# Second matrix of the early expert: loaded into the first one's buffers as they are split, split behind the token table

## The chip, the cores and the metric

One core of a Trainium2 chip runs one program. Its engines work side by side, each through a queue of its own: TensorE (PE, with its weight loads PEld), VectorE (DVE), ScalarE (ACT), GpSimd (POOL) and SyncE (SP), which here issues nearly all transfers between memory and the core's buffers. The metric is the device time of the program in microseconds (us), the median of the timed runs.

## The reference: what is computed

Three stages follow each other on 2304 tokens (4 batches x 576 positions) of 512 features:

```python
# attention: a downsampled one (mean of 4 positions) and a local band of +-3 positions
out_up = np.repeat(sm_attn(q_d, k_d, v_d), 4, axis=2)
out_local = np.matmul(softmax(mask(scale * q @ k.T)), v)
x = out_up + out_local                       # -> (2304, 512)
# mixture of 8 experts, one per token
logits = x @ w_gate + modality_bias[modality_id]
e_idx = np.argmax(logits, axis=1); gate_w = softmax(logits)[e_idx]
for e in range(8):                           # w1: 512x1024, w2: 1024x512 each
    out[mask] = gate_w * (np.maximum(x[mask] @ w1[e], 0.0) @ w2[e])
# dense layer, 512 -> 2048 -> 512, with softplus between
g = np.maximum(h, 0.0) + np.log1p(np.exp(-np.abs(h)))   # h = x @ w_in
return g @ w_out
```

All tensors are float32.

## The kernel before

**Precision and splits.** A float32 product is made of three products: each operand is split into a high part `wh` (an ACT copy into a shorter type, L332) and a low part `wl` (a DVE subtraction of `wh` from the raw value, L333). A weight matrix of an expert (2 MB) is loaded and split in four *quarters* of 128 x 1024 values (512 KB). A quarter is loaded by SP into one of eight raw buffers, raw0 to raw7, split from there into a ring of `wh`/`wl` pairs, and the raw buffer is then free for the next load.

**Slots.** Behind the gate the tokens are gathered by expert into slots of 128 rows. A slot s runs `gemm1` (24 matmuls against w1, `h` = its result behind a ReLU, L582), `h_t` (PE turns h, L1149; ACT and DVE split it into `hh` and `hl`, L526 and L527) and `gemm2` (24 matmuls against w2; ACT writes the result `y`, L1170, SP stores it to `ys`, L1172). Slots 0 and 1 belong to the *early expert*: the one with the most tokens after half of them have been gated. Its w1 is loaded and split while the attention of the last tokens still runs (step "W" of phase A), and its 8 quarters serve both slots. From slot 2 on the expert comes from a table `widx` that the last gate group makes. SP reads `widx` into registers (L283, for two mixed slots L311) and issues the loads under a condition (L289, L290), which leaves a load out where a slot has the same expert as the one before.

**The order.** The list `parts` gives the order in which quarters are loaded and split: parts 0 to 3 are the early expert's w1, 4 to 7 its w2, 8 to 11 w1 of slot 2, 12 to 15 w1 of slot 3, 16 to 19 w2 of slot 2, and so on. Products ask for their quarters through `part`, which splits up to two quarters ahead; `split_part` also loads up to eight ahead as far as buffers are free. The function `raw_of` says which raw buffer a quarter uses: in the slots w1 takes raw4 to raw7 and w2 raw0 to raw3. The buffers raw4 to raw7 exist from the start; raw0 to raw3 belong to a pool that opens behind phase A. Within one engine's queue a scheduler may move instructions by its own estimate, except those that are marked with `keep_in_program_order`, which keep their order among themselves.

**The last gate group.** The tokens 13*128 to 18*128 are the last gate group. For a tile PE turns x (L833), ACT copies it (`xT`, L834), PE multiplies it with the gate's weights (L845), ACT copies that (`lT`, L847), PE collects (L848); DVE then makes the logits (`lg`, L861), the maximum (`gmx`, L864), `ex` (L867) and the counts; PE sums them (L888), and DVE goes on to the token table (`tokt`, L935) and to `widx` (L412). `tables` turns the token table into the lists `gidx` by which POOL gathers the slots' rows (`xg`, L521). The attention's loads `up` (L767, added to x by POOL, L821) are in SP's queue at the same time.

Of the kernel before, what the change touches and what calls it, by code (L numbers as in the profile page):

```python
# [19 lines left out]
def tile_attention_moe_ffn(  # L20
# [37 lines left out]
    SM = 20  # L58
# [16 lines left out]
    NR = (4, 8)  # L75
    NRT = sum(NR)
    PIN = 24
    GP = 4
    PL = 8
# [11 lines left out]
    def f32(t):  # L91
        return t.bitcast(F32)
# [132 lines left out]
    where = {}  # L225
# [7 lines left out]
    def raw_of(kind, s, j):  # L233
        if kind == 3:
            return s if s < 4 else 4 + s % 4
        return j if s >= SM else (kind % 2) * 4 + j

    def add_parts(kind, s):
        for j in range(4):
# [23 lines left out]
    def load_part(i):  # L263

        kind, s, j = parts[i]
        at = raw_of(kind, s, j)
        if at not in raws or owner.get(at, i) not in split and at in owner:
            return False
        owner[at] = i
        t = raws[at]  # L270
        if kind == 3:
            x = sp.dma_start(out=t, in_=wf[s])
            if NR[0] <= s < 8:
                tc.keep_in_program_order(x)
        else:
            w = w1r if kind == 1 else w2r
            if s < NSTAT:
                if "star" not in eids:
                    eids["star"] = sp.value_load(star_i[0:1, 0:1], min_val=0, max_val=NE - 1)
                sp.dma_start(out=t, in_=w[bass.ds(eids["star"] * DM + j * 128, 128), :])  # L280
            else:
                if s not in eids:
                    eids[s] = sp.value_load(widx[0:1, dix[s]:dix[s] + 1], min_val=0, max_val=2 * NE - 1)  # L283
                e = eids[s]
                r = (e & (NE - 1)) * DM + j * 128
                if s >= SM:
                    sp.dma_start(out=t, in_=w[bass.ds(r, 128), :])
                else:
                    with tc.If(e < NE):  # L289
                        sp.dma_start(out=t, in_=w[bass.ds(r, 128), :])  # L290
        loaded.add(i)
        return True
# [8 lines left out]
    def load_mixed(i):  # L301

        kind, s, j = parts[i]
        at = ring_of(i)
        w = w1r if kind == 1 else w2r
        ts = []
        for a, nm in enumerate(("wh", "wl")):
            t = ring[at].tile([128, 1024], F32, tag=nm, name=nm, bufs=NR[at])
            d = NDF + 2 * MIX.index(s) + a
            if (s, a) not in eids:  # L310
                eids[s, a] = sp.value_load(widx[0:1, d:d + 1], min_val=0, max_val=NE - 1)  # L311
            sp.dma_start(out=t, in_=w[bass.ds(eids[s, a] * DM + j * 128, 128), :])
            ts.append(t)
        split[i] = ts

    def split_part(i):
        for n in range(i, min(i + 8, state["end"], FF0 + CD)):
            if parts[n][1] in MIX and parts[n][0] < 3:
                continue
            if n not in loaded and not load_part(n):  # L320
                break
        if parts[i][1] in MIX and parts[i][0] < 3:
            return load_mixed(i)
        at = ring_of(i)
        if at < 2:
            hi = ring[at].tile([128, 1024], F32R, tag="wh", name="wh", bufs=NR[at])
            lo = ring[at].tile([128, 1024], F32R, tag="wl", name="wl", bufs=NR[at])
        else:
            hi, lo = extra.pop(0)
        assert i in loaded or i >= FF0 + CD  # L330
        r = raws[raw_of(*parts[i])]
        ins = (act.activation(out=hi, in_=r, func=ACTF.Copy),  # L332
               dve.tensor_tensor(out=lo, in0=r, in1=f32(hi), op=ALU.subtract))  # L333
        if PL <= i < PIN or i < NR[0]:
            tc.keep_in_program_order(ins[1])
            tc.keep_in_program_order(ins[0])
        if i >= FF0:
            for x in ins:
                tc.keep_in_program_order(x)
        split[i] = (hi, lo)  # L340
# [245 lines left out]
    def phase_a(actx):  # L586
# [423 lines left out]
        def step(t, what):  # L1010
            if what == "LV":
                for x in range(nv[0], min(t + LVA, NTT - 1) + 1):
                    load_v(x)
                    nv[0] += 1
            elif what == "LG" and t in LGT:
                load_vg(LGT.index(t) + 1)
            elif what == "S" and t < NTT:
                local_s(t)
            elif what == "E" and t < NTT:
                local_e(t)  # L1020
            elif what == "T" and 0 <= t - 1 < NTT:
                local_t(t - 1)
            elif what == "O" and 0 <= t - OL < NTT:
                local_o(t - OL)
                done_o.add(t - OL)
            elif what == "P":
                prep_to(PS(t))
            elif what == "DN":
                for b in sorted({b for b, _ in dnew}):
                    down_q(b)  # L1030
                dunits.extend(dnew)
                dnew.clear()
            elif what == "DS":
                for _ in range(min(DN, len(dunits))):
                    d_s.append(dunits.pop(0))
                    down_s(*d_s[-1])
            elif what == "DT":
                for x in d_s:
                    down_t(*x)
                d_t.extend(d_s)  # L1040
                d_s.clear()
            elif what == "DO":
                for x in d_t:
                    down_o(*x)
                    if x[1] == 1:
                        pooled.add(x[0])
                d_t.clear()
            elif what == "LU":
                for _ in range(UN):
                    x = q_lu[0]  # L1050
                    if x in done_o and batches[x] <= pooled:
                        load_up(x)
                        q_u.append(x)
                        q_lu[0] += 1
            elif what == "U":
                for x in q_u:
                    local_up(x)
                q_x.extend(q_u)
                q_u.clear()
            elif what == "X":  # L1060
                for x in q_x:
                    x_T(x, gof[x])
                q_m.extend(q_x)
                q_x.clear()
            elif what == "M":
                for x in q_m:
                    gate_mm(x, gof[x])
                    if x == gof[x][-1]:
                        q_g.append(gate(gof[x]))
                q_m.clear()  # L1070
            elif what == "XT":
                x_t(0, bka)
            elif what == "F":
                next(first, None)
            elif what == "G":
                for g in list(q_g):
                    x = next(g, 1)
                    if x == 1:
                        q_g.remove(g)
            elif what == "W" and picked and q_pr[0] == NTT:  # L1080
                if not ring:
                    bctx.close()
                    ring.append(ctx.enter_context(tc.tile_pool(name="ring0", bufs=NR[0], side="right", reuse_waits="tile")))
                    xps.append(cctx.enter_context(tc.tile_pool(name="xp", bufs=3, side="right", reuse_waits="tile")))
                    xps.append(cctx.enter_context(tc.tile_pool(name="h1", bufs=1, side="right", reuse_waits="tile")))
                    with tc.issue_after(lastq[0].ins):
                        for j in range(4):
                            load_part(j)
                if gather_now:
                    gather_now.clear()  # L1090
                    gather_x(0)
                    gather_x(1)
                if ws[0] < 4 and t >= WT + ws[0]:
                    split_part(ws[0])
                    ws[0] += 1
            elif what == "Z" and t == 1:
                build_bias(cA, cB)
            elif what == "Z" and t == 10:
                zero = raws[7][:, 0:YW]
                tc.keep_in_program_order(pool.memset(zero, 0.0))  # L1100
                for s in range(SM, NS):
                    tc.keep_in_program_order(pool.dma_start(out=ys[s * 128:(s + 1) * 128, :], in_=zero))

        nv = [1]
        ws = [0]
# [8 lines left out]
        def PS(t):  # L1114
            return PSL[t] if t < len(PSL) else t + 5
# [17 lines left out]
    def phase_cd():  # L1133
# [139 lines left out]
        next(tb)  # L1273
        state["end"] = bounds[0]
        for j in range(4):
            load_part(where[2, 0, j])
        for j in range(4):
            split_part(where[2, 0, j])
        TB = 6
        G0 = 14  # L1280
# [146 lines left out]
```

## Time and profile before

| what | us |
|---|---|
| median of 3 runs (918.93 to 923.62) | 922.46 |
| profiled execution, its own time | 925.12 |
| its span on the core | 923.4 |
| PE busy in the span | 853.3 |
| DVE busy | 654.7 |
| ACT busy | 547.1 |

The page gives each engine's busy time as a sum over the whole span. Views of a stretch show more: a list of one engine's instructions in order of time, where a row names its start, its duration, the line and operation, the tile written and the tiles read, and in brackets how long the engine was idle ahead of it and what ended that wait; and a table of stretches with each engine's busy time in them. DMA issues of SP are rows of its queue; their duration is that of the issue, not of the transfer. Buffer numbers are left out in names, and both w1 and w2 are `in_moe_w_dram`. Attention and gate end near 217 us, the slots run from there to about 490 us, the dense layer to the end.

### The profile page before, as it was taken

To read this page: it belongs to the slowest core of one execution; us is meant where nothing else is said; L and a number is where in the kernel's file an instruction comes from. 1 tells how busy PE (TensorE), PEld (TensorE's weight loads), DVE (VectorE), ACT (ScalarE), POOL (GpSimd) and SP (SyncE) were. 2 spreads that over 40 slices of the span, in tenths; PEclk is the share of its full clock that TensorE was granted. 3 is DMA by queue.
4 is the path that set the end of the run, shared out by engine and by line. 5 is a ranking of instruction groups with operands and counts; after the bars stand their busy time and mean duration, and the time that the engine had idled before them with its cause. 6 is when DMAs were issued, how large, how long until landed. Compare 5 with 4: busy or idle time off the path is not lost. (4 is left out here: it accounts for less than half of the span.)

```text
span 923.4 us, 15325 instructions
## 1 busy us (share of the span) xinstructions
PE 853.3 (92%) x5356; PEld 725.9 (79%) x5356; DVE 654.7 (71%) x1271; ACT 547.1 (59%) x935; POOL 214.8 (23%) x263
## 2 busy tenths in 40 slices
PE   6797899868899999999999999899999999999996
PEld 6687788756777766786687898789899998999984
DVE  6576487678699988976857798656656665666662
ACT  3553564453699777876857677656545555455451
POOL 8322554230243342511001222202000000000001
PEclk9998899799999999999999999999999999999999
DMA  9999785672934599577354333202001001000000
GB/s 164 191 174 195 171 199 126 177 194 94 309 123 138 175 368 332 205 265 252 115 194 147 99 94 109 69 12 65 27 12 35 23 12 34 24 12 12 24 1 34
DMA packets 109112, 115.68 MB, mean 125 GB/s; under 512 B 68448, under 2 KB 83552, under 8 KB 109024
## 3 DMA queue, kind: packets, MB, share of 16 engines
q1 hardware_dynamic: 101072, 98.28, 38.0%
q0 software_dynamic: 4960, 16.28, 5.5%
q8 instruction: 44, 0.72, 0.3%
q10 hardware_dynamic: 2992, 0.04, 0.2%
q14 instruction: 44, 0.36, 0.1%
HBM read 92.93 MB, written 21.65 MB: 124 GB/s over the span
## 5 line engine op out<-in xcount | busy, mean ns | idle before, releaser
L333 DVE TENSOR_TENSOR wl<-raw,wh 128x1024 fp32r<-128x1024 f32 x152 | 187.6, 1256 | 34.8 <-ACT wh L332 31.8
L332 ACT ACTIVATE wh<-raw 128x1024 fp32r<-128x1024 f32 x152 | 159.2, 1064 | 39.8 <-DMA raw<-in_moe_w_dram 16.7
L552 PE MATMUL p<-yh,wh 128*128 128x384 f32 x384 | 131.6, 343 | 11.3 <-DVE e L1239 10.1
L556 PE MATMUL p<-yh,wl 128*128 128x384 f32 x384 | 129.4, 337 | 0.0
L555 PE MATMUL p<-yl,wh 128*128 128x384 f32 x384 | 129.3, 337 | 0.0
L552 PE MATMUL p<-wh,gh 128*128 128x512 f32 x288 | 113.8, 395 | 1.1 <-ACT gh L1244 1.1
L555 PE MATMUL p<-wl,gh 128*128 128x512 f32 x288 | 113.2, 393 | 0.0
L556 PE MATMUL p<-wh,gl 128*128 128x512 f32 x288 | 101.4, 395 | 0.1
L1238 ACT ACTIVATE u<-u 128x384 f32<-128x384 f32 x96 | 50.1, 524 | 80.1 <-DVE e L1237 80.1
L552 PEld LDWEIGHTS p<-yh,wh 128*128 128x128 f32 x384 | 72.1, 188 | 18.7 <-DVE e L1239 14.2
L1245 DVE TENSOR_TENSOR gl<-e,gh 128x384 fp32r<-128x384 f32 x96 | 57.5, 600 | 40.7 <-ACT gh L1244 39.9
L1244 ACT ACTIVATE gh<-e 128x384 fp32r<-128x384 f32 x96 | 50.1, 523 | 45.1 <-DVE e L1240 44.8
L555 PEld LDWEIGHTS p<-yl,wh 128*128 128x128 f32 x384 | 72.2, 188 | 3.0
L1231 ACT ACTIVATE e<-p 128x384 f32<-128x384 f32 x96 | 46.4, 488 | 46.3 <-PE p L556 42.8
L556 PEld LDWEIGHTS p<-yh,wl 128*128 128x128 f32 x384 | 72.1, 188 | 0.3
L1192 POOL DMA_INDIRECT yg<-ys,pos x18 | 19.1, 1060 | 216.4 <-PE p L1209 205.7
L1237 DVE SCALAR_TENSOR_TENSOR e<-u,e 128x384 f32<-128x384 f32 x96 | 55.2, 577 | 13.4 <-ACT u L1234 11.2
L556 PEld LDWEIGHTS p<-wh,gl 128*128 128x128 f32 x288 | 54.0, 188 | 12.9 <-DVE gl L1245 0.8
L552 PEld LDWEIGHTS p<-wh,gh 128*128 128x128 f32 x288 | 54.1, 188 | 10.5 <-ACT gh L1244 1.5
L1240 DVE TENSOR_TENSOR e<-e,u 128x384 f32<-128x384 f32 x96 | 55.3, 579 | 9.0 <-ACT u L1238 1.3
L555 PEld LDWEIGHTS p<-wl,gh 128*128 128x128 f32 x288 | 54.2, 188 | 8.7
L552 PE MATMUL p<-wh,hh 128*128 128x512 f32 x144 | 58.9, 409 | 1.8 <-ACT y L1170 1.5
(256 smaller groups left out, 1800.4 us busy)
## 6 DMA issues: line engine op xcount, KB each, us to landing
raw<-in_moe_w_dram SPq DMA_DIRECT2D x40, 512.0 KB
cv<-in_moe_w_in_dram SPq DMA_DIRECT2D x16, 512.0 KB
cv<-in_moe_w_out_dram SPq DMA_DIRECT2D x16, 512.0 KB
wh<-in_moe_w_dram SPq DMA_DIRECT2D x16, 512.0 KB
wl<-in_moe_w_dram SPq DMA_DIRECT2D x16, 512.0 KB
vw<-in_v_dram SPq DMA_DIRECT2D x36, 144.0 KB
ys<-y SPq DMA_DIRECT2D x20, 256.5 KB
vg<-in_v_dram SPq DMA_DIRECT2D x16, 288.0 KB
```

Of the source, the lines that this page charges most:

```text
L332: ins = (act.activation(out=hi, in_=r, func=ACTF.Copy), dve.tensor_tensor(out=lo, in0=r, in1=f32(hi), op=ALU.subtract))
L333: dve.tensor_tensor(out=lo, in0=r, in1=f32(hi), op=ALU.subtract))
L552: i = pe.matmul(out=ps, lhsT=lh, rhs=rh, start=first, stop=False)
L555: pe.matmul(out=ps, lhsT=lh, rhs=rl, start=False, stop=False)
L556: pe.matmul(out=ps, lhsT=ll, rhs=rh, start=False, stop=last)
L1192: pool.indirect_dma_start(out=y, out_offset=None, in_=ys[0:rows], in_offset=bass.IndirectOffsetOnAxis(ap=pos[:, t:t + 1], axis=0))
L1231: act.activation(out=e, in_=ps, func=ACTF.Abs)
L1237: dve.scalar_tensor_tensor(out=e, in0=u, scalar=-1.0, in1=e, op0=ALU.add, op1=ALU.subtract)
L1238: act.activation(out=u, in_=u, func=ACTF.Ln)
L1240: dve.tensor_tensor(out=e, in0=e, in1=u, op=ALU.add)
L1244: act.activation(out=gh, in_=e, func=ACTF.Copy)
L1245: dve.tensor_tensor(out=gl, in0=e, in1=f32(gh), op=ALU.subtract)
```

## The change

The second matrix of the early expert, parts 4 to 7, moves in two ways. Its four loads leave the place behind phase A: each is now issued in step "W", right behind the split of the w1 quarter whose buffer it takes, so w2 is loaded into raw4 to raw7 as well. Its four splits stay where they are in the code, behind the token table's first step (`next(tb)`), but the condition on `keep_in_program_order` now covers them too (all parts below 24), so that the scheduler can't move them ahead of other marked instructions. With that, `raw_of` exchanges the buffers of the later slots: w1 of a slot takes raw0 to raw3, w2 raw4 to raw7.

```diff
     def raw_of(kind, s, j):
         if kind == 3:
             return s if s < 4 else 4 + s % 4
-        return j if s >= SM else (kind % 2) * 4 + j
+        return j if s >= SM or kind == 1 and s else 4 + j
...
-        if PL <= i < PIN or i < NR[0]:
+        if i < PIN:
             tc.keep_in_program_order(ins[1])
             tc.keep_in_program_order(ins[0])
...
                 if ws[0] < 4 and t >= WT + ws[0]:
                     split_part(ws[0])
+                    load_part(where[2, 0, ws[0]])
                     ws[0] += 1
...
         tb = tables(tbp)
         next(tb)
         state["end"] = bounds[0]
-        for j in range(4):
-            load_part(where[2, 0, j])
         for j in range(4):
             split_part(where[2, 0, j])
```

**ACT, end of the last gate group.** Before, with the splits of w2 in raw0 to raw3 among the gate's copies:

```order
L834 ACTIVATE xT_2947<-b1_2948 128x512
L332 ACTIVATE wh_3176<-raw0_3123 128x1024
L834 ACTIVATE xT_2954<-b1_2955 128x512
L847 ACTIVATE lT_2966<-b1_2961 128x128
L332 ACTIVATE wh_3180<-raw1_3124 128x1024
L847 ACTIVATE lT_2974<-b1_2969 128x128
L332 ACTIVATE wh_3184<-raw2_3125 128x1024
L332 ACTIVATE wh_3188<-raw3_3126 128x1024
L868 ACTIVATE ex_2990<-ex_2990 128x40
L582 ACTIVATE h_2977<-b1_2978 128x512
```

After, at the same place and on to the token table's copies `t0`:

```order
L834 ACTIVATE xT_2951<-b1_2952 128x512
L834 ACTIVATE xT_2958<-b1_2959 128x512
L847 ACTIVATE lT_2970<-b1_2965 128x128
L847 ACTIVATE lT_2978<-b1_2973 128x128
L868 ACTIVATE ex_2994<-ex_2994 128x40
L582 ACTIVATE h_2981<-b1_2982 128x512
...
L459 ACTIVATE t0_3140<-p6_3137 16x128
L332 ACTIVATE wh_3176<-raw4_86 128x1024
L332 ACTIVATE wh_3180<-raw5_87 128x1024
L332 ACTIVATE wh_3184<-raw6_88 128x1024
L332 ACTIVATE wh_3188<-raw7_89 128x1024
```

The four splits of w2 moved from among the gate's copies to behind the token table; on DVE their other halves moved likewise, from among the steps `lg`, `gmx` and `ex` to behind the casts of `gidx`.

**SP, from slot 2's last w1 load on.** Before, the reads of `widx` (10 of them at the first "...", then 2, 2 and 3 ahead of the next three loads) stand between the loads, and the store `ys` of slot 0's result `y` behind all of them:

```order
L290 DMA raw7_89<-in_moe_w1_dram 128x1024
L283 TENSOR_LOAD widx_90
...
L290 DMA raw4_86<-in_moe_w1_dram 128x1024
...
L290 DMA raw5_87<-in_moe_w1_dram 128x1024
...
L290 DMA raw6_88<-in_moe_w1_dram 128x1024
...
L290 DMA raw7_89<-in_moe_w1_dram 128x1024
...
L290 DMA raw0_3123<-in_moe_w2_dram 128x1024
...
L290 DMA raw3_3126<-in_moe_w2_dram 128x1024
...
L1172 DMA ys_64<-y_3365 128x513
```

After, with all 19 reads at the first "...":

```order
L290 DMA raw3_3130<-in_moe_w1_dram 128x1024
L283 TENSOR_LOAD widx_90
...
L290 DMA raw0_3127<-in_moe_w1_dram 128x1024
...
L290 DMA raw1_3128<-in_moe_w1_dram 128x1024
...
L290 DMA raw2_3129<-in_moe_w1_dram 128x1024
...
L1173 DMA ys_64<-y_3365 128x513
...
L290 DMA raw3_3130<-in_moe_w1_dram 128x1024
...
L290 DMA raw4_86<-in_moe_w2_dram 128x1024
...
L290 DMA raw7_89<-in_moe_w2_dram 128x1024
```

All reads of `widx` moved ahead of slot 3's first w1 load, and the store of y ahead of its fourth one and of slot 2's w2.

**ACT, slot 0's result.** Before, `y` and the first half of `hh` of slot 1 stand ahead of the splits of slot 3's w1:

```order
L582 ACTIVATE h_3226<-p1_3228 128x512
...
L1170 ACTIVATE y_3365<-p5_3299,gw_2913 128x512
L526 ACTIVATE hh_3369<-p3_3371 128x512
L526 ACTIVATE xh_3293<-p2_3288 128x512
L332 ACTIVATE wh_3310<-raw4_86 128x1024
L332 ACTIVATE wh_3331<-raw5_87 128x1024
```

After:

```order
L582 ACTIVATE h_3226<-p1_3228 128x512
L526 ACTIVATE xh_3293<-p2_3288 128x512
...
L332 ACTIVATE wh_3310<-raw0_3127 128x1024
...
L332 ACTIVATE wh_3331<-raw1_3128 128x1024
L526 ACTIVATE hh_3369<-p3_3371 128x512
L1171 ACTIVATE y_3365<-p5_3299,gw_2917 128x512
L526 ACTIVATE hh_3369<-p4_3378 128x512
```

`y` and `hh` moved behind the splits of the first two quarters of slot 3's w1.

## Rows read from the trace of the kernel before

**Rows 1.** Page, busy time of the engines over the whole span:

```profile
PE 853.3 (92%) x5356; PEld 725.9 (79%) x5356; DVE 654.7 (71%) x1271; ACT 547.1 (59%) x935; POOL 214.8 (23%) x263
```

**Rows 2.** Table of stretches: busy time by engine, PE's clock, DMA share, GB/s:

```profile
200.00:205.00 5.00, 0.36 (x9) 0.10 (x8) 0.58 (x4) 1.29 (x2) 0.00 (x0) 0.84 0.92 269
```

**Rows 3.** ACT in order of time, last gate group (start, duration, instruction, idle ahead):

```profile
203.71 1.06 ACT L332 ACTIVATE wh<-raw 128x1024 fp32r<-128x1024 f32 x1 [5.41 <-DMA raw<-in_moe_w_dram]
204.67 0.58 ACT L834 ACTIVATE xT<-b 128x512 f32<-128x512 f32 x1
```

**Rows 4.** PE in order of time, from the gate to slot 2:

```profile
205.31 0.66 PE L845 MATMUL b<-xT,wg 128*32 128x128 f32 x8 [4.94 <-ACT xT L834]
...
211.57 0.17 PE L888 MATMUL b<-cacc,ones 128*128 128x8 bf16 x1 [1.62 <-DVE cacc L882]
...
236.49 0.66 PE L533 MATMUL p<-ident,xg 128*128 128x128 f32 x4 [1.13 <-DMA xg<-xs,gidx]
...
248.83 0.40 PE L556 MATMUL p<-wh,hl 128*128 128x512 f32 x1
250.97 1.23 PE L1149 MATMUL p<-ident,h 128*128 128x128 f32 x8 [1.74 <-ACT h L582]
```

**Rows 5.** DVE in order of time, the last two gate groups:

```profile
197.42 2.09 DVE L926 TENSOR_SCALAR ohc<-iotac,cf,rank 128x144 fp32r<-128x144 f32 x4
...
206.40 1.23 DVE L333 TENSOR_TENSOR wl<-raw,wh 128x1024 fp32r<-128x1024 f32 x1 [0.37 <-ACT wh L332]
207.54 0.19 DVE L861 TENSOR_TENSOR lg<-b,biast 128x40 f32<-128x40 f32 x1
...
210.02 0.19 DVE L867 TENSOR_TENSOR ex<-lg,gmx 128x40 f32<-128x40 f32 x1
...
218.92 0.17 DVE L412 SCALAR_TENSOR_TENSOR widx<-up 128x28 int32<-128x28 f32 x1
```

**Rows 6.** SP's queue in order of time: issues of weight loads, slots 2 and 3:

```profile
219.80 0.34 SPq L290 DMA_DIRECT2D raw<-in_moe_w_dram  x1
220.67 1.17 SPq L290 DMA_DIRECT2D raw<-in_moe_w_dram  x2
222.42 0.33 SPq L290 DMA_DIRECT2D raw<-in_moe_w_dram  x1
229.75 0.35 SPq L290 DMA_DIRECT2D raw<-in_moe_w_dram  x1
231.94 0.34 SPq L290 DMA_DIRECT2D raw<-in_moe_w_dram  x1
...
236.86 0.34 SPq L290 DMA_DIRECT2D raw<-in_moe_w_dram  x1
...
240.53 0.33 SPq L290 DMA_DIRECT2D raw<-in_moe_w_dram  x1
```

**Rows 7.** ACT in order of time, splits of slots 2 and 3:

```profile
223.31 1.06 ACT L332 ACTIVATE wh<-raw 128x1024 fp32r<-128x1024 f32 x1 [0.41 <-DMA raw<-in_moe_w_dram]
225.96 1.06 ACT L332 ACTIVATE wh<-raw 128x1024 fp32r<-128x1024 f32 x1 [1.59 <-DMA raw<-in_moe_w_dram]
228.03 1.06 ACT L332 ACTIVATE wh<-raw 128x1024 fp32r<-128x1024 f32 x1 [1.01 <-DMA raw<-in_moe_w_dram]
229.29 1.06 ACT L332 ACTIVATE wh<-raw 128x1024 fp32r<-128x1024 f32 x1 [0.20 <-DMA raw<-in_moe_w_dram]
...
234.97 0.69 ACT L1170 ACTIVATE y<-p,gw 128x512 f32<-128x512 f32 x1 [3.65 <-issue]
...
249.37 1.06 ACT L332 ACTIVATE wh<-raw 128x1024 fp32r<-128x1024 f32 x1 [1.09 <-DMA raw<-in_moe_w_dram]
250.34 1.06 ACT L582 ACTIVATE h<-p 128x512 f32<-128x512 f32 x2
```

**Rows 8.** POOL in order of time: the add of the loads `up`:

```profile
185.10 2.51 POOL L821 TENSOR_TENSOR x<-x,up 128x512 f32<-128x512 f32 x2 [0.78 <-DMA up<-upd]
```

**Rows 9.** Instructions of line L283: count, shortest, median and longest in ns:

```profile
L283 SPq TENSOR_LOAD <-widx x16: 261/268/279, 219.1 to 241.7; - x16
```

## Prediction

> **What bounds the kernel now.** TensorE (PE) sets the time: it is busy for 853.3 of 923.4 us [rows 1], so the change can only be worth what it does to PE's idle time. Cut into stretches of 5 us, the emptiest one late in the attention phase is 200 to 205 us, with 0.36 us of PE work [rows 2]. The reader finds its cause in ScalarE's (ACT) list [rows 3]: the first split of w2 (L332) starts at 203.71 after 5.41 us of waiting for its DMA, and behind it in ACT's queue stands the copy L834 of the last token tile, at 204.67. PE's L845 needs that copy and starts at 205.31 after 4.94 us idle [rows 4]. In VectorE's (DVE) list the other halves of the four splits (L333) stand among the small steps of the last gate group: one ends at 207.63, just ahead of the step lg (L861, 207.54), and two more stand between lg and ex (L867, 210.02) [rows 5]. The gate then leads to PE's count L888 at 211.57 [rows 4], to the table widx (218.92, [rows 5]) and to SyncE's (SP) first weight load that depends on it, at 219.80 [rows 6].
>
> From there the limit is another one: quarters of weights. ACT waits for a quarter at 223.31, 225.96 and 229.29, and for the last quarter of slot 2's w2 at 249.37; only behind that one it copies h (L582, 250.34) [rows 7], and PE turns h (L1149) at 250.97 after 1.74 us idle [rows 4]. I carry the sum to that point, because both kernels have done the same work there, and after it the same slots follow.
>
> **The change part by part.** *The gate.* Four splits leave it. ACT's L834 need no longer wait for a DMA, but PE's transpose before it (L833) now stands behind four table matmuls (L932) whose operands DVE makes until 199.51 (197.42 and 2.09, [rows 5]); so L834 runs at about 200.7 instead of 204.67, a gain of 4.0. One split of 1.06 us [rows 3] that stands on ACT between the two copies lT behind it, and the half on DVE that ends ahead of lg, go: 1.1. From lg to ex 210.02 - 207.54 = 2.5 us pass with two halves between; without them some 0.2 are left for gmx: 2.3. Together 7.4 us at L888.
>
> *The earlier loads.* Each of the four issues (about 0.34 us) stands in SP's queue where its buffer's split has just ended, so SP waits little. But the second is in the queue ahead of the attention's loads `up`, and POOL's add already waits 0.78 us for those, at 185.10 [rows 8]. A quarter takes 2.0 us when quarters follow each other ((229.29 - 223.31) / 3, [rows 7]). So this costs the last token tile between 0 (the transfer fits in the gap) and 2.0; PE's L932 hides some 0.8 of it, and I take 0.5. A second 0.4 goes because DVE now does tokt ahead of widx. That leaves 6.5 us: SP's first load of slot 2's w1 at 213.3 instead of 219.80. By the same spacing as before its quarters are there at 216.8 to 222.8 and cause no new wait.
>
> *The splits in their new place.* Four of them, 4 x 1.06 on ACT and 4 x 1.2 on DVE [rows 3, 5], now lie between the token table and slot 2's splits. PE has 24 matmuls of slot 1 to do there, so slot 0's second product finds its quarters split. But DVE reaches them only after the casts of gidx, which wait for PE's table matmuls (L462 to L470) inside slot 1's first product, so slot 2's w1 is split, and its buffers raw0 to raw3 come free, at 227.5 to 231.
>
> *SP's queue.* This is where I expect the gain to go. Before, 10 reads of widx (L283, L311) stand between slot 2's last w1 load at 222.42 and slot 3's first at 229.75, and the other 9 lie among the next loads: 2, 2 and 3 of them ahead of the next three, and 2 behind [rows 6]. After, all 19 stand ahead of slot 3's first load. Two reads and a load took 231.94 - 229.75 = 2.19, a load alone 0.91 ((240.53 - 236.86) / 4), so a read costs 0.64 (the instruction itself 0.27, [rows 9]). Hence: last load of slot 2 at 213.3 + 2.6 = 215.9, then 7.33 as before, and 9 x 0.64 = 5.8 more: 229.0. That is only 0.8 earlier than 229.75: 5.8 of the 6.5 us are given back. Slot 3's next two quarters follow at 229.9 and 230.9.
>
> *The store y.* SP's fourth load of slot 3, and all four of slot 2's w2, stand after the change behind the store of slot 0's result (ys). ACT makes that y only behind the splits of slot 3's first two quarters and the copy hh; before, y came ahead of them, at 234.97 [rows 7]. The second quarter, issued at 229.9, lands after 5.3 us if it does as the second of slot 2 did (220.67 to 225.96, [rows 6, 7]): at 235.2, I take 235.0. Then split 1.06, hh 0.5, y 0.7, ys 0.6: the fourth load goes at 237.9, against 236.86 before. Five quarters from there take 3.5 for the first (219.80 to 223.31) and 4 x 2.0: the last lands at 249.4, against 249.37. On ACT one half of h now stands ahead of the last split, so PE's second four transposes start at about 251.0 (249.4, the split's 1.06 and half of h, 0.5), against some 251.5 (250.97 and half of their 1.23). PE itself is done with the rest earlier: it stops at 232, takes up slot 1's second product when hh is there at 236.7, and needs 10.9 more (12.7 us of work ran from 236.49 to 249.23 before, [rows 4], of which transposes and four matmuls worth 1.9 are done already): 247.6. So it waits there.
>
> **The sum:** 6.5 gained, 5.8 back to the reads of widx, 0.7 back to y and the transfers, 0.5 gained at h: 0.5 us less, a span of 922.9 for 923.4, and about 924.6 for the profiled execution's 925.12. The three runs have a median of 922.46, 2.66 below it, so I expect **922.0 us**. The rest of the slots is reordered only in small ways (the late loads of the first FFN quarters go a little earlier, PE waits for none of them), at 0, within 1.5 either way.
>
> **The rivals.** *The DMAs keep up.* The last two of slot 2's quarters came 1.26 apart (228.03 and 229.29, [rows 7]). With less queued than before, five quarters at 1.26 are there at 246.5, and PE's own 247.6 decides: 3.3 us gained, 919.2. Against it: quarters before that point landed up to 8.8 us after their issue (240.53 to 249.37, [rows 6, 7]). The Trainium skill (DMA: Bandwidth & Descriptors, Specifications) gives about 358 GB/s of HBM for one core; by that, as an estimate, 512 KB take 1.46 us, and the same rival would win, with the last quarter at about 247.2. The rows with 2.0 apart speak against the page's figure here.
>
> *The gain stays.* If the 19 reads do not line up as I count them (a read's own 0.27 us instead of 0.64 saves 19 x 0.37 = 7.0 us of SP's time), slot 3's loads are bound by their buffers at 227.5, y comes 1.5 earlier, and if the quarters follow quickly as well, 4.8 to 6.5 us are kept: 916.0 to 917.7. Against it stands 0.64 in every gap of the trace.
>
> *Slower, by the queue of ACT.* ACT holds hh and y behind two quarters. If the second one lands 8.8 us after its issue, as the last one did before, it is there at 238.7, and everything behind (y, five loads, h) comes 3.7 later: 926.2. The point from which this decides is a landing at 235.5, hardly later than my 235.0. For it speaks that nothing else can pass on ACT or SP; against it, that the gathers of x, which shared the DMAs with slot 3's quarters before, now go at about 220, ahead of them.
>
> *Slower, by the early loads.* If three quarters in front of the `up` loads each delay the last tiles by 2.0, less the 0.8 hidden, the gate ends only 2 us earlier and all behind it slips by 5: 927.5.
>
> **How the numbers follow.** My forecast has a chance of 0.50, the DMAs keeping up 0.18, the gain kept 0.14, ACT's queue 0.12, the early loads 0.06. About 0.5% (4.6 us) is what a measurement of this kernel can tell from no change: below 917.85 lie the kept gain and a little of the second case, 0.17; above 927.07 the early loads and the far end of ACT's queue, 0.10; between them 0.73. The range of 916.5 to 926.5 leaves out the outer part of the kept gain and the early loads.
>
> **What would show it.** Right: ACT has no wait of 5 us near 200; L888 at 204 to 205.5; widx's first load at 212.5 to 214; a gap of some 13 us in SP's loads behind the fourth, with slot 3's first at 228 to 230; y at 236 to 238 instead of 234.97, with PE idle some 4 us ahead of it; L1149's third group (L1150 after) near 250. Wrong: slot 3's first load before 226, which would keep the gain; y before 234; or L888 later than 207.

## The result, and the profile after

| | before | after |
|---|---|---|
| median, us (6 runs each) | 920.30 (915.15 to 923.62) | 931.83 (928.31 to 936.15) |
| profiled execution, us | 925.12 | 929.31 |
| its span, us | 923.4 | 927.6 |

After stands to before as 1.0121, with a 95% interval of 1.0087 to 1.0155: the change makes the kernel slower by 11.5 us, outside the forecast range. The profiled execution of before (925.12) is slower than all six of these runs (at most 923.62) and that of after is the second fastest of its own six, so these two traces show only 4.2 us of the 11.5. What makes the whole of it is tested by medians, in the experiments.

First the part that the prediction followed, beside [rows 1 to 7]. The page's busy time, the stretch of 200 to 205 us, ACT's and PE's last steps of the gate in after:

```profile
PE 855.1 (92%) x5356; PEld 725.1 (78%) x5356; DVE 657.3 (71%) x1271; ACT 546.2 (59%) x935; POOL 221.9 (24%) x263
```

```profile
200.00:205.00 5.00, 3.98 (x40) 2.68 (x39) 2.48 (x18) 1.28 (x4) 0.00 (x0) 1.00 0.17 56
```

```profile
200.50 0.60 ACT L834 ACTIVATE xT<-b 128x512 f32<-128x512 f32 x1 [2.45 <-PE b L833]
```

```profile
204.48 0.17 PE L888 MATMUL b<-cacc,ones 128*128 128x8 bf16 x1 [0.55 <-DVE cacc L882]
235.66 0.79 PE L552 MATMUL p<-wh,hh 128*128 128x512 f32 x1 [5.86 <-ACT y L1171]
...
248.56 1.11 PE L1150 MATMUL p<-ident,h 128*128 128x128 f32 x8
```

The hole of [rows 2] is filled: PE is busy for 3.98 of the 5 us instead of 0.36, ACT no longer waits for a DMA ahead of L834, and the count L888 comes at 204.48 instead of 211.57. Then SP's weight loads of slots 2 and 3, and the quarters' splits and y on ACT:

```profile
212.72 1.28 SPq L290 DMA_DIRECT2D raw<-in_moe_w_dram  x2
...
227.87 1.34 SPq L290 DMA_DIRECT2D raw<-in_moe_w_dram  x2
...
236.43 0.34 SPq L290 DMA_DIRECT2D raw<-in_moe_w_dram  x1
```

```profile
231.30 1.06 ACT L332 ACTIVATE wh<-raw 128x1024 fp32r<-128x1024 f32 x1 [6.08 <-DMA raw<-in_moe_w_dram]
233.49 1.06 ACT L332 ACTIVATE wh<-raw 128x1024 fp32r<-128x1024 f32 x1 [1.13 <-DMA raw<-in_moe_w_dram]
...
234.93 0.68 ACT L1171 ACTIVATE y<-p,gw 128x512 f32<-128x512 f32 x1
...
240.70 1.06 ACT L332 ACTIVATE wh<-raw 128x1024 fp32r<-128x1024 f32 x1 [3.66 <-DMA raw<-in_moe_w_dram]
242.07 1.06 ACT L332 ACTIVATE wh<-raw 128x1024 fp32r<-128x1024 f32 x1 [0.32 <-DMA raw<-in_moe_w_dram]
243.38 1.06 ACT L332 ACTIVATE wh<-raw 128x1024 fp32r<-128x1024 f32 x1 [0.25 <-DMA raw<-in_moe_w_dram]
244.66 1.06 ACT L332 ACTIVATE wh<-raw 128x1024 fp32r<-128x1024 f32 x1 [0.22 <-DMA raw<-in_moe_w_dram]
...
246.47 1.06 ACT L332 ACTIVATE wh<-raw 128x1024 fp32r<-128x1024 f32 x1 [0.26 <-DMA raw<-in_moe_w_dram]
```

The first load is 7.1 us earlier than in [rows 6], the fifth only 1.9 (227.87 for 229.75): the reads of widx give the rest back, as forecast. PE waits 5.86 us for y (some 4 were forecast), and the transposes of slot 2's h (L1150) start at 248.56 instead of 250.97 [rows 4]. At y of slot 3 after is 3.1 us ahead (276.07 for 279.21).

One pair of executions does not settle a lead of this size. Five of the versions below, all on after (the mixed products, the third buffer, the deeper buffers, the conversion left out, the conversion fixed), have after's order in the queues of ACT, DVE, POOL and SP until 276 us. In these five and after itself slot 2's transposes start between 247.25 and 252.10 us, at 249.75 in the mean. In before and the two versions on it with before's order until 272 us (the conversion left out, the conversion fixed) they start between 248.67 and 250.97, at 249.86 in the mean. For y of slot 3 the means are 277.33 and 278.09. So up to here the two kernels are about even, and of the 6.2 us that L888 is earlier in the mean hardly anything is left.

So the loss is made later. The starts of y, one row of ACT in each slot, show where. The first and the last that are compared, before and then after:

```profile
279.21 0.68 ACT L1170 ACTIVATE y<-p,gw 128x512 f32<-128x512 f32 x1
...
490.69 0.69 ACT L1170 ACTIVATE y<-p,gw 128x512 f32<-128x512 f32 x1 [1.94 <-PE p L556]
```

```profile
276.07 0.68 ACT L1171 ACTIVATE y<-p,gw 128x512 f32<-128x512 f32 x1
...
495.83 0.69 ACT L1171 ACTIVATE y<-p,gw 128x512 f32<-128x512 f32 x1 [1.93 <-PE p L556]
```

| y of slot | before | after | after is late by | gained or lost since the row above |
|---|---|---|---|---|
| 3 | 279.21 | 276.07 | -3.1 | |
| 4 | 292.45 | 292.03 | -0.4 | lost 2.7 |
| 5 | 305.86 | 306.70 | 0.8 | lost 1.3 |
| 6 | 320.06 | 320.67 | 0.6 | gained 0.2 |
| 8 | 346.67 | 351.04 | 4.4 | lost 3.8 |
| 19 | 490.69 | 495.83 | 5.1 | lost 0.8 |

The three larger losses have their rows. In the slots from 4 on a piece of work goes on that neither the diff nor the prediction names: the *conversion* of the dense layer's weights from pairs of 32-bit words to float32. One step of it is a load `cv` by SP, an ACT copy into `cm` (L206), two steps on DVE (L209, L213), an add on POOL that reads `cm` (L215) and a store `wf` by SP. `cm` has two buffers. The program's text asks for one or two steps in each slot from 8 on; the scheduler sets each engine's order by its own estimate, and pulls them up to four slots ahead. This is ACT's list and PE's around 290 us, after:

```profile
290.04 0.66 ACT L206 ACTIVATE cm<-cv 128x512 int32<-128x512 uint32 x1 [3.59 <-POOL cz L215]
290.61 1.04 ACT L332 ACTIVATE wh<-raw 128x1024 fp32r<-128x1024 f32 x1
291.55 0.58 ACT L526 ACTIVATE hh<-p 128x512 fp32r<-128x512 f32 x1
292.03 0.68 ACT L1171 ACTIVATE y<-p,gw 128x512 f32<-128x512 f32 x1
```

```profile
292.76 0.50 PE L552 MATMUL p<-wh,hh 128*128 128x512 f32 x1 [3.05 <-ACT y L1171]
307.43 0.50 PE L552 MATMUL p<-wh,hh 128*128 128x512 f32 x1 [1.83 <-ACT y L1171]
```

ACT's copy into `cm` waits 3.59 us for a buffer that POOL has not yet read, hh and y stand behind it, and PE stops for 3.05 us. Near 307 the same happens again. In before PE's waits at these two places were 0.35 and 0.56, and ACT's copy found its buffer free:

```profile
289.51 0.68 ACT L206 ACTIVATE cm<-cv 128x512 int32<-128x512 uint32 x1
```

```profile
293.21 0.50 PE L552 MATMUL p<-wh,hh 128*128 128x512 f32 x1 [0.35 <-ACT y L1170]
```

The difference is POOL's order, after and then before:

```profile
282.53 6.16 POOL L521 DMA_INDIRECT xg<-xs,gidx  x1 [9.06 <-PE p L552]
288.71 2.51 POOL L215 TENSOR_TENSOR cz<-cz,cm 128x512 int32<-128x512 int32 x2
```

```profile
285.42 2.12 POOL L215 TENSOR_TENSOR cz<-cz,cm 128x512 int32<-128x512 int32 x1 [0.72 <-DVE cz L213]
287.69 1.77 POOL L521 DMA_INDIRECT xg<-xs,gidx  x1
```

After, a gather of x stands ahead of the adds, and takes 6.16 us; before it stood behind the add and took 1.77.

The third loss is on PE itself. The mixed slot 9 multiplies with two weight matrices, each half of the array with its own (L561, 32 half-width matmuls in the first product: `wh` and `wl` are the two experts' quarters here). Before, and then after:

```profile
338.91 0.64 PE L561 MATMUL p<-wh,xh 128*64 128x512 f32 x1
338.92 0.64 PE L561 MATMUL p<-wl,xh 128*64 128x512 f32 x1
339.39 0.59 PE L561 MATMUL p<-wh,xh 128*64 128x512 f32 x1
339.40 0.59 PE L561 MATMUL p<-wl,xh 128*64 128x512 f32 x1
```

```profile
336.82 1.88 PE L561 MATMUL p<-wh,xh 128*64 128x512 f32 x4
338.63 0.33 PE L533 MATMUL p<-ident,xg 128*128 128x128 f32 x1
338.89 1.93 PE L561 MATMUL p<-wl,xh 128*64 128x512 f32 x4
```

Before, a matmul of `wh` and one of `wl` start together and a pair takes 0.43 to 0.48 us. After, the scheduler has put full-width matmuls (transposes, and two of slot 8's second product) between the `wh` and the `wl` of the last two quarters; four of one half then take 1.88 to 1.93 us, each about as long as a pair before, and the 16 that are left need 7.6 us (4 x 1.9) instead of 8 pairs x 0.43 = 3.4: some 4.2 us lost.

### The profile page after: what moved, and what is told of

It reads as the page before. It is cut to its first block, busy times and chain, and to the rows that moved or that the text cites. A ratio compares the mean times of both kernels' runs of the same rounds, so it can differ in the third digit from the quotient of the medians.

```text
span 927.6 us, 15337 instructions
## 1 busy us (share of the span) xinstructions
PE 855.1 (92%) x5356; PEld 725.1 (78%) x5356; DVE 657.3 (71%) x1271; ACT 546.2 (59%) x935; POOL 221.9 (24%) x263
## 5 line engine op out<-in xcount | busy, mean ns | idle before, releaser
L333 DVE TENSOR_TENSOR wl<-raw,wh 128x1024 fp32r<-128x1024 f32 x152 | 194.4, 1302 | 32.0 <-ACT wh L332 31.2
L1246 DVE TENSOR_TENSOR gl<-e,gh 128x384 fp32r<-128x384 f32 x96 | 55.3, 577 | 41.7 <-ACT gh L1245 40.7
L521 POOL DMA_INDIRECT xg<-xs,gidx x20 | 45.4, 2270 | 105.3 <-PE p L533 24.3
```

The lines of the kernel that those rows point to most:

```text
L521: pool.indirect_dma_start(out=t, out_offset=None, in_=xs[0:TG0 * 128] if s < NSTAT else xs, in_offset=bass.IndirectOffsetOnAxis(ap=gidx[:, ...
L1246: dve.tensor_tensor(out=gl, in0=e, in1=f32(gh), op=ALU.subtract)
```

## The experiments

Two theories went into the first four runs. A: the loss is made by the order that the scheduler sets in the slots 7 to 9 once the four splits are fixed. B: it is made by the earlier loads and the exchanged buffers. All ratios are to the kernel before in the same runs.

**The fixed order of the four splits alone**, on before:

```diff
-        if PL <= i < PIN or i < NR[0]:
+        if i < PIN:
```

> Kernel before with one part of the change alone: the condition on the fixed order (the splits of parts 4 to 7 are kept in order); loads and buffers stay as before. Theory A (the loss comes from the order that the scheduler makes for slots 7 to 9 once these four splits are fixed): the products of slot 9 are cut up by full-width matmuls as after the change, PE waits for y near 290 and 305, and the time is 929 to 933, 1.0 to 1.4% above before. Rival B (the loss comes from the earlier loads and the exchanged buffers): 918 to 922, as before or a little below.

Measured: 925.9, ratio 1.0081 (1.0054 to 1.0109). Its order on ACT and POOL is that of after, and so are the cut product of slot 9 and the wait near 290 (near 307 PE waits only 0.48):

```profile
293.08 0.80 PE L552 MATMUL p<-wh,hh 128*128 128x512 f32 x1 [2.57 <-ACT y L1170]
```

It is slower than before without any moved load, which B doesn't give; but it lies below the range of A.

**The rest of the change without the fixed order**, on after:

```diff
-        if i < PIN:
+        if PL <= i < PIN or i < NR[0]:
```

> Kernel after without the fixed order of parts 4 to 7: the four early loads and the exchanged buffers alone; the splits go back among the gate's copies, but no longer wait for a DMA there. Theory A: the 5.4 us wait near 204 is gone, y stands ahead of the splits of slot 3 again, one cut remains in slot 9's first product (2 us), so 917 to 922, about 11 below after. Rival B: 929 to 933, as after.

Measured: 930.45, ratio 1.0120 (1.0101 to 1.0139). A falls as I had put it: this half alone costs as much as the whole change, as B has it. But its trace has the loss at another place. Until y of slot 9 it is 4.8 us behind before, then one interval (y of slot 9 to y of slot 10) takes 19.8 us instead of 13.9. DVE's list and PE's there:

```profile
384.06 0.43 DVE L209 TENSOR_SCALAR cy<-cv 128x512 int32<-128x512 int32 x1 [2.75 <-DMA cv<-in_moe_w_in_dram]
...
385.53 0.69 DVE L213 SCALAR_TENSOR_TENSOR cz<-cv,cy 128x512 int32<-128x512 int32 x1
...
387.27 0.68 DVE L527 TENSOR_TENSOR xl<-p,xh 128x512 fp32r<-128x512 f32 x1
```

```profile
388.01 1.22 PE L556 MATMUL p<-wh,xl 128*128 128x512 f32 x2 [6.86 <-DVE xl L527]
```

Again a step of the conversion, here one that waits for its own load, stands in an in-order queue ahead of what PE needs; its wait of 2.75 us is a part of PE's 6.86. So the place differs and the kind is the same. That gave theory D: whatever edit makes the scheduler plan anew, the steps of the conversion fall on new places in the queues of ACT, DVE and POOL, and PE pays where one of them waits.

**The mixed products kept together**, on after (the same mark goes on slot 10's transposes and on the first matmuls of slot 8's second product):

```diff
-            pe.matmul(out=ps[ph], lhsT=L[:, ph], rhs=R[a], start=first, stop=last)
+            tc.keep_in_program_order(pe.matmul(out=ps[ph], lhsT=L[:, ph], rhs=R[a], start=first, stop=last))
```

> Kernel after with the matmuls of the mixed slots' products kept together (fixed order on PE: the 32 half-width matmuls of slot 9's first product stand in a row, and the next transposes and slot 8's second product come behind them). Theory A: the 32 take 16 pairs x 0.43 = 6.9 us instead of about 11, 4.1 us come back: 927.5 to 928, 0.4% below after. If half-width matmuls do not run beside each other, or if something else holds PE there (the weights of slot 9, the gather of slot 10): no difference to after, 931.8.

Measured: 939.26, ratio 1.0225 (1.0197 to 1.0254): slower, not faster. The trace shows both. From y of slot 6 to y of slot 8 it takes 26.0 us, against 30.4 in after and 26.6 in before: the 32 matmuls run in pairs again and 4.4 us come back, as worked out. But the new mark set yet another order. From y of slot 8 to y of slot 13, with new waits near 375 to 380 us, 3.1 are lost on after, and between y of slots 13 and 14 the program takes 21.9 us instead of 15.4, where PE meets a gather (`yg`) that now comes late, and then works at the lower clock (0.50 granted from 424 to 430) with pairs 0.85 us apart:

```profile
424.24 1.09 PE L1210 MATMUL p<-ident,yg 128*128 128x128 f32 x4 [3.41 <-DMA yg<-ys,pos]
```

**A third buffer for cm**, on after; the order of ACT, DVE, POOL and SP stays as it was:

```diff
-            m = cvp[-1].tile([128, DM], I32, tag="cm", name="cm")
+            m = cvp[-1].tile([128, DM], I32, tag="cm", name="cm", bufs=3 if c < CD else None)
```

> Kernel after with three buffers instead of two for cm (the conversion's ACT copy, L206), so that this copy need not wait for POOL's add of two conversions before; the order of all instructions stays that of after. Theory A (ACT's wait for POOL, 3.59 and 1.74 us near 290 and 305, holds up y and with it PE): L206 has no wait for POOL there, PE's idle times of 3.05 and 1.83 at L552 shrink to under 0.6 each, and 3 to 4.5 us come back: 927.5 to 929. If DVE, which is busy without a gap from 250 to 320, holds PE anyway: within 1 us of after, 931 to 932.5.

Measured: 929.05, ratio 1.0109 (1.0086 to 1.0132), some 2 to 3 us below after, less than its interval can tell. The wait for POOL near 290 is gone, and with it PE's 3.05 (y of slot 3 to slot 4: 12.5 us instead of 16.0). In its place the next step waits, near 297 us:

```profile
288.35 0.68 ACT L206 ACTIVATE cm<-cv 128x512 int32<-128x512 uint32 x1
...
296.87 0.68 ACT L206 ACTIVATE cm<-cv 128x512 int32<-128x512 uint32 x1 [4.34 <-SPq L289]
```

Here ACT waits for the copy's load, which left SP only at 292.28, behind a store `wf` that waited for POOL's add. From y of slot 4 to slot 5 it takes 16.1 us instead of 14.7, and PE's wait near 307, which was to shrink, stays at 1.89. One wait removed lets the next one come forward.

**The conversion's arithmetic left out**, on after and on before:

```diff
+            if c < CD:
+                sp.dma_start(out=wf[c, :, j * DM:(j + 1) * DM], in_=cz0[0])
+                return
```

> Kernel after without the arithmetic of the weights' conversion in the slots (L206, L209, L213, L215 left out; the transfers in and out remain, zeros are stored, so the first half of the dense layer's weights is left out of the result). Compared with the run without conversion of the kernel before. Theory D (the loss comes from the conversion's steps: they stand in the queues of ACT, DVE and POOL at places that a scheduler sets anew with every edit, wait there for transfers or for POOL, and hold up y, hh and xl behind them): without them the slots 3 to 19 take the same time in both kernels within 1 us, and the lead of about 3 us that after has at slot 3 is kept: after is 1 to 4 us below before. Rival B (moved loads, exchanged buffers): after stays 8 or more above before.

> Kernel before with the same left out (the arithmetic of the conversion in the slots; zeros are stored for the first half of the dense layer's weights). Theory D: slots 3 to 19 lose PE's waits at y and xl, a few us below before (912 to 918), and 1 to 4 above the same of after. Rival B: 8 or more below it.

Measured, both with an incomplete result: after without the arithmetic 913.78, ratio 0.9909 (0.9880 to 0.9939); before without it 914.63, ratio 0.9945 (0.9913 to 0.9977). The first stands to the second as 0.9964, give or take 0.0044. Of the 11.5 us of loss nothing is left; whether the change then gains anything can't be told. The time from y of slot 3 to y of slot 19, read from ACT's rows (after, then before):

```profile
279.62 0.68 ACT L1175 ACTIVATE y<-p,gw 128x512 f32<-128x512 f32 x1
...
481.94 0.69 ACT L1175 ACTIVATE y<-p,gw 128x512 f32<-128x512 f32 x1 [1.94 <-PE p L560]
```

```profile
276.90 0.68 ACT L1174 ACTIVATE y<-p,gw 128x512 f32<-128x512 f32 x1
...
483.42 0.69 ACT L1174 ACTIVATE y<-p,gw 128x512 f32<-128x512 f32 x1 [1.91 <-PE p L560]
```

is 202.3 and 206.5, where it was 219.8 in after and 211.5 in before. So leaving it out saves 5 us in before and 17 in after. That is not the price of the conversion alone, since the order is a new one in both; theory D's "within 1 us" is missed, by 4.2, of which 2.53 are a wait of PE for xl in the version on before, at 345.90. (That the version on after reaches y of slot 3 late, at 279.6, is a difference between executions: up to there its queues hold after's order.)

**y of slot 0 first**, on after: the second product of slot 0 asks for no quarter ahead.

```diff
-        n = 2
+        n = 0 if kind == 2 and s == 0 else 2
```

> Kernel after in which slot 0's second product asks for no quarter ahead, so that y of slot 0 and hh of slot 1 stand ahead of the splits of slot 3 in ACT's queue; the order from there on is that of after. If y behind those splits costs what the trace shows (PE idle 5.86 us at 229.8, then the clock low until 240, the fourth load of slot 3 at 236.43): y at 229.5, SP's fourth load at 231 to 232, slot 2's h 4 to 6 us earlier, and 926 to 928. If the quarters' transfers or VectorE's work on the later slots bind anyway: within 1.5 of after (930.5 to 933).

Measured: 929.46, ratio 1.0085 (1.0057 to 1.0113). y goes at 230.63 and PE's 5.86 us are gone, but PE then waits at slot 2's h, and y of slot 1 is only 0.9 earlier than in after:

```profile
246.09 0.74 PE L1150 MATMUL p<-ident,h 128*128 128x128 f32 x4 [3.76 <-ACT h L582]
```

The measured time lies between the two answers, nearer to the second. That the quarters bind here, as the second has it, fits the row but was not tested: five loads leave SP from 232.70 on, one behind another.

**Deeper buffers**, on after: three of each tile of the conversion, its loads one step further ahead.

```diff
-t = cvp[-1].tile([128, DM, 2], I32, tag="cv", name="cv", bufs=2)
+t = cvp[-1].tile([128, DM, 2], I32, tag="cv", name="cv", bufs=3 if c < CD else 2)
...
+                    if s == TB + 1:
+                        conv_load()
...
-tc.tile_pool(name="cvc", bufs=2, side="right", reuse_waits="tile")
+tc.tile_pool(name="cvc", bufs=3, side="right", reuse_waits="tile")
```

> Kernel after with three buffers instead of two for each of the conversion's tiles and its loads one step further ahead; all its arithmetic is kept. Theory D: the conversion's steps find their data and their buffers, L206 and L209 wait for no transfer and not for POOL, PE's waits at y and xl between 285 and 400 go, and 920 to 925 are reached. If it is not the waits but the work itself (VectorE is busy without a gap from 250 to 320 in both kernels): 928 to 933.

Measured: 926.26, ratio 1.0059 (1.0039 to 1.0080), between the two answers: 5.6 us below after. With more buffers the scheduler pulls the steps still further ahead, PE still stops (4.14 us at 302.35 for hl), and only from y of slot 9 on is it faster than before (122.4 us to y of slot 19, for 127.2).

**The conversion fixed at its place**, on after and on before: its copy (L206) and its first DVE step (L209) keep program order against y, so that none can be pulled ahead of the slot that asks for it. All arithmetic is there.

```diff
-            if c >= CD:
-                tc.keep_in_program_order(i1)
+            tc.keep_in_program_order(i1)
...
+            if TB <= s < SM:
+                for x in i:
+                    tc.keep_in_program_order(x)
```

> Kernel after with the conversion's steps on ACT and DVE (L206, L209) kept in program order against y (its copy on ACT and its cast on DVE), so that the scheduler can't pull them four slots ahead: one or two conversions in each slot from 8 to 19 instead of all between 275 and 395 us. All arithmetic is kept. Theory D (conversion steps in the queues of the slots 4 to 12 are what costs): slots 3 to 19 take 202 to 206 us as without conversion (219.76 in after), and 914 to 920 is reached. If the conversions cost PE the same wherever they stand, or the last ones now come too late for the dense layer: 925 or more.

> Kernel before with the same fixed order of the conversion. Theory D: 915 to 920, and 1 to 3 above the same of after, since only the early part of the change is then left between them. Rival B (moved loads, exchanged buffers cost by themselves): 8 or more below it.

Measured: after with the fixed conversion 920.73 (just above D's 914 to 920), ratio 1.0009 (0.9986 to 1.0032); before with it 919.09, ratio 0.9986 (0.9961 to 1.0012). After gets 11 us faster by that, before hardly, and between them 1.0023 remains, give or take 0.0035: no difference. From 250 us on POOL's order is then the same in both, and ACT's but for one place near 290. B, by which after should have stayed 8 or more above, is out: the moved loads and exchanged buffers cost nothing by themselves that these runs can tell. The y of slot 3 and of slot 19 in both (after first):

```profile
276.74 0.68 ACT L1169 ACTIVATE y<-p,gw 128x512 f32<-128x512 f32 x1
...
487.17 0.69 ACT L1169 ACTIVATE y<-p,gw 128x512 f32<-128x512 f32 x1 [1.94 <-PE p L554]
```

```profile
278.16 0.68 ACT L1168 ACTIVATE y<-p,gw 128x512 f32<-128x512 f32 x1
...
488.24 0.69 ACT L1168 ACTIVATE y<-p,gw 128x512 f32<-128x512 f32 x1 [1.93 <-PE p L554]
```

210.4 and 210.1 us: the slots now cost the same in both. The hoped-for 202 to 206 didn't come: y is at 447.53 in slot 16 of the changed kernel, 11.1 us ahead of before, and 7.6 of these go in the last slots, where PE stops for 4.41 us until 471.00.

**Both edits at once**, on after:

> Both edits at once on the kernel after: the conversion's fixed order, and slot 0's second product without quarters ahead (y of slot 0 first). Theory: y first gave 0.9 us at slot 1's y by the profiles and about 2 in the medians, so 0 to 3 below the version with the fixed order alone; if the quarters of slot 2 bind, the same within 1.

Measured: 917.38, ratio 0.9977 (0.9952 to 1.0003), 3.3 below the fixed order alone, at the edge of the 0 to 3 expected. The two traces don't show where it comes from: y of slot 19 is at 487.23 here and at 487.17 there.

**And the conversions done by slot 17**:

```diff
-for _ in range((2 if s % 3 == 0 else 1) if TB < s < SM else 0):
+for _ in range((2 if s in (9, 11, 13, 15, 16, 17) else 1) if TB < s < SM else 0):
```

> As the version with both edits (fixed order of the conversion, slot 0's y first), but the sixteen conversions are done by slot 17 instead of slot 19 (two each in slots 9, 11, 13, 15, 16 and 17), so that the stores of converted weights no longer stand in SP's queue ahead of the weight loads of slots 17 and 18. If the gap of 21 us between the results y of slots 16 and 17 comes from those stores (13.6 us in the kernel before): 4 to 8 us less, 910 to 914. If two conversions in a slot hold up PE again, as in the kernel after: 917 or more.

Measured: 917.62, ratio 0.9957 (0.9922 to 0.9992), 4.6 us below before in the same runs and some 1.6% below after. It is the one version with the whole result whose interval lies below before, if barely; against the version before it nothing can be told. The 910 to 914 were missed: from y of slot 16 to y of slot 17 it still takes 20.5 us (PE's one long stop there, until 467.92, is 2.94 us). ACT waits there for a quarter of weights:

```profile
460.57 1.06 ACT L330 ACTIVATE wh<-raw 128x1024 fp32r<-128x1024 f32 x1 [6.70 <-DMA raw<-in_moe_w_dram]
```

SP issues these loads at 454.84, behind two stores of converted weights (446.81) and the dense layer's first quarters. What would bring them forward wasn't tried.

## Why the prediction was wrong

**The gate, right.** L888 was to come 7.4 us earlier and came 7.1 earlier, at 204.48 (6.2 in the mean of the executions named above).

**The earlier loads, right.** SP's first load of slot 2 was put at 213.3; it goes at 212.72 (213.20 in the mean). The gate's gain arrives there, so the attention's last tiles are not held up by more than the forecast allowed.

**SP's queue, right in kind.** Slot 3's first load was put at 229.0 and goes at 227.87; the fourth at 237.9 and goes at 236.43. The reads of widx take back 5.2 of 7.1 us, where the sum had 5.8 of 6.5.

**The store y and the transfers, mis-sized in part.** y goes at 234.93, where the terms (quarter at 235.0, split, hh) make 236.6: its quarter was there at 233.49. In the mean of the six executions y goes at 236.07, so that term holds. But the quarters behind it came 1.3 apart (240.70 to 244.66, in four splits), not 2.0: here the first rival, that the DMAs keep up, was right in its mechanism. It put the last split at 246.5, and it is at 246.47; that this agrees so well is luck, since the fourth load went 1.5 us earlier than in its sum, the first quarter took 4.3 us instead of 3.5, and the last came 1.8 behind its neighbour. By the figure that the Trainium skill gives (DMA: Bandwidth & Descriptors, Specifications, some 358 GB/s of HBM for a core) an estimate of 1.46 us a quarter was nearer than my 2.0, and the rows of 1.3 are a little faster still. At slot 2's h the two kernels stand 2.4 us apart in this pair and 0.1 in the means, where I had 0.5: the sum up to this point was right, within what executions differ.

**The rest of the slots, wrong.** This is the step that failed: "reordered only in small ways, at 0, within 1.5 either way". Measured from y of slot 3 to y of slot 19 it costs 8.3 us (219.8 for 211.5): 2.7 and 1.3 where y stands behind a waiting step of the conversion, 3.8 around slot 9's cut product, 0.8 in the rest, 0.2 gained between. With a front that is about even in the means, that leaves some 3 to 5 of the 11.5 us for which no trace shows a place. I had carried the sum to slot 2's h "because both kernels have done the same work there, and after it the same slots follow". The same slots do follow, but in another order, and ACT, DVE and POOL each work their queue in order. The two rivals on the slower side named early places (ACT's queue at slot 3, the `up` loads); the mechanism that decided, new places for work that the diff doesn't touch, was none of them, so its chance had no share of its own.

Shown by runs: the loss needs the conversion's arithmetic (without it after is no slower), and it goes when the conversion is fixed at its place (with all its arithmetic). Both edits set a new order too, but luck of the order is a weak rival: the four versions with the conversion fixed lie at 917.38 to 920.73, after and the six other versions with all arithmetic and the conversion not fixed at 925.9 to 939.26; of the orders that were not fixed, only before's own is as fast. Nor can it be just that conversion steps fall where VectorE is busy without a gap (10.00 of 10 us in each ten from 260 to 310, in both kernels): before has its 16 copies at 275.2 to 376.8, after at 277.6 to 384.7. Shown by rows, not by a run that changes it alone: that POOL's order delays ACT's copy near 290. The cut product, 3.8 of the 8.3 us, is no wait for a conversion step. But the product is whole again both in after without the arithmetic and in after with the fixed conversion (26.8 and 26.7 us from y of slot 6 to y of slot 8), so it too hangs on where the scheduler puts the conversion, in a way that no row shows. Open: why the fixed order of the splits alone (1.0081) costs less than the whole change (1.0121); the intervals overlap.

## What to carry to other kernels

Where a scheduler orders the queues, an edit at one place moves work everywhere: lay the order of the whole program before and after side by side, look for steps that can wait (for a transfer, for a slow engine) and have come to stand ahead of what the bounding engine needs, and price each one, however far from the edit. Fix background work, such as a conversion of later weights, at its place against the steps that matter, before judging any other edit; otherwise a measurement may mostly measure the new shuffle. A gain near the front is worth nothing by itself until the stages behind it keep it. And before reading a lead of 2 or 3 us from one trace, look at the same row in other executions with the same order: here they lie up to 4.9 us apart.

## What the hardware showed beside that

**POOL's gathers.** The issue of a gather (L521) takes 0.94 to 2 us on POOL at most places, but 7.67, 3.01, 6.16, 5.43 and 4.83 in after between 256 and 320, and before has 8.82 at 258.49 and 5.30 at 385.01. During all of these VectorE is busy for 96% of the time or more (10.00 of 10 us from 280 to 290, and again from 290 to 300). That alone doesn't make a gather slow: before's at 287.69 and 299.30 took 1.77 and 1.80 us with VectorE as busy; what decides is not shown. The other way round, the split on DVE beside POOL's adds of 288.71 took 3.93 us instead of 1.2:

```profile
288.39 3.93 DVE L333 TENSOR_TENSOR wl<-raw,wh 128x1024 fp32r<-128x1024 f32 x1
```

The extra 2.7 us are about the 2.51 of the two adds. The Trainium skill (GPSIMD Engine Reference, Specifications) says that GpSimd shares its SBUF interfaces with VectorE and contends with instructions that have two SBUF inputs, as L333 has; the row of the split agrees, and adds what it costs.

**Half-width matmuls.** That two halves of the array work at the same time is what the Trainium skill says (TensorEngine Tiling (Array Packing), Key Properties), and 0.43 us for a pair agrees. New is what takes it away: where four matmuls of one half stand in a row, with full-width ones between them and the four of the other half, each of the eight needs about as long as a pair (1.9 us for four).

**The clock.** After PE's stop of 5.86 us the clock was granted at its lower level (1.2 GHz) for the next stretch, whose matmuls take 0.63 us instead of 0.40; the row gives PE's busy time first, and the granted clock, 0.50, third from the end:

```profile
235.00:240.00 5.00, 4.34 (x10) 3.47 (x11) 3.23 (x4) 2.04 (x4) 0.00 (x0) 0.50 0.61 163
```

So this stop cost more than itself: the ten matmuls start 0.43 us apart instead of 0.23, which is 2.0 us. Not every stop did: after the 3.05 us until 292.76 the granted clock stayed at 1.00 (292.8 to 297.8).
